# Where a transform group takes its PSUM banks: the two banks of the x products in mid-step, or one of them and a scratch bank at the step's end

## The chip, the cores and the metric

The kernel runs on one core of a Trainium2 chip. The metric is device time in microseconds. The engines are named as in the profile: PE is TensorE (its matmuls), PEld its weight loads, DVE VectorE, ACT ScalarE, POOL GpSimd, SP SyncE. "L255" is line 255 of the kernel.

## What is computed

```python
# x: (8, 3008, 256)   w_in: (256, 2048)   w_out: (2048, 256), all float32
X = np.fft.fft(x, axis=1)
X = np.fft.fft(X, axis=2)
x = X.real.astype(np.float32).reshape(8 * 3008, 256)
h = x @ w_in
g = h * (1.0 / (1.0 + np.exp(-1.702 * h)))
out = (g @ w_out).astype(np.float32)
```

## The kernel before

All arithmetic is in float32. The Fourier transform over the sequence (3008 = 47 x 64) is done in two stages of matmuls, one batch ahead of the rest; the transform over the 256 features is folded into `w_in` beforehand. What remains is a two-layer network with a gated activation, whose products are cut down by the symmetries of the transform and by Strassen-like combinations.

**Steps.** The network runs in 384 steps t: 8 batches, 3 blocks of a batch, 2 halves of a block, 8 pairs p = t mod 8 of feature blocks. A step with (block 0, half 1) has 226 columns ("narrow"), every other 256 ("wide"). Steps 0 to 7 use a simpler form; from step 8 on a loop written out by hand (`for t in range(n + LAG)`) issues the work, and every engine takes its instructions in that order. LAG is 3: the products with `w_out` of step t - 3 are issued in step t. The parts of a step are these:

- `middle(t)`, ACT, L592, two instructions: writes a bias into the PSUM bank `b{t % 2}`, the bank of x(t).
- `begin(t)` (called P here) and `begin(t, 1)` (called Q), PE, L184 by way of `halves`, output `x`: two groups of eight matmuls each that add the two halves of the products of step t onto that bias. P(t + 1) is issued in the middle of step t, Q(t) at the start of step t.
- `doubled(t)`, ACT, L604: reads x(t) after P. `forward(t)`, ACT, L607: reads x(t) after Q. `backward(t)`, DVE, L565 (one instruction, two in narrow steps): reads x(t) and the result of `doubled`, the last to read the bank. `activate_back(t)`, ACT, L614.
- `sums(t)`, POOL, L622 and L623, and DVE, L629 and L630; `deeper`, DVE, L651: sums from which the products with `w_out` are made. `deeper` follows odd steps.
- `product(t - 3, lo, hi)`, PE, L184, output `o` or `low`: the halves lo to hi of a step's products. From step 8 up to the last eight a step has three halves, of four matmuls each.
- `small_products(t, ks)`, PE, L685: sets of eight small matmuls, only for odd t: sets 1, 2, 4, 7 of t - 3 (`one`) and sets 5, 6, 3 of t - 4 (`other`).
- Once in eight steps a group of outputs is put together: `combine` (ACT L754, L756, DVE L757, L758), `combine_small` (DVE L786, in steps with t mod 8 = 3), `swap` (ACT L794 to L796, three copies, in steps with t mod 8 = 4), `combine_last` (DVE L768, L804).

A step with t mod 8 = 3 is "opening": it issues the first products of an output group.

**Transform groups.** The two stages of the transform for the next batch or block are spread over the steps by a table `extra`, whose entries are called at a step's end. `mix1` (PE L255, 16 to 22 matmuls, two PSUM banks) is followed by two copies by `mixed` (ACT, L263); `stage2` (PE L365, 64 small matmuls, two PSUM banks) by four transposes (DVE, L371). `mix1` needs what `fold1` (POOL, L225 to L231) made. There are 28 `mix1` and, from step 8 on, 23 `stage2`, in 51 steps that the code calls `special`; `after` is a step whose predecessor was special. In batches 1 to 6 (t0 = 48 b) `mix1` comes in steps t0 + 12, 15, 19 and 23, in batch 0 in 16, 20, 25 and 28; `stage2` comes in t0 + 8, 24 and 40.

**Banks.** PSUM has eight banks: two for `o`, three for `low`, `b0` and `b1` for x, and `b2`. A function that asks `bank(name)` without a tag takes the first of the list `spare`. A bank is handed over when the instructions that read its former content are done:

```python
def middle(t):
    x = xb[t] = bank("x", f"b{t % 2}")
    ...
def mix1(b, m):
    ps = [bank("ps1") for _ in range(2)]
    ...                        # matmuls into ps[0] and ps[1] in turn
    waiting.append((m, ps[1]))
    mixed(m, 0, ps[0])
```

Before, a special step s sets `spare` to `b{s % 2}` and `b2`: the group is issued at the end of step s, into the bank of x(s), which `middle(s + 2)` would have taken, and the scratch bank. `middle(s + 2)` is then issued in the after step, behind Q(s + 1). In other steps `middle(t + 2)` is issued in step t.

Of the kernel before, what the change touches and what calls it, by code (L numbers as in the profile page):

```python
# [43 lines left out]
LAG = 3  # L44
# [68 lines left out]
def kernel(ctx: ExitStack, tc, x, w_in, w_out, tab1, tab2, out):  # L113
    nc = tc.nc
# [147 lines left out]
    def mixed(m, r, ps):  # L262
        nc.scalar.copy(free(xt[:], (4 * m + r) * D, [2 * D, 2], [1, D]), free(ps[:], 0, [D, 2], [1, D]))  # L263
# [321 lines left out]
    def middle(t):  # L585

        b, blk, hh, p = steps[t]
        n = width(t)
        x = xb[t] = bank("x", f"b{t % 2}")
        for i in range(2):  # L590
            f = 2 * p + i
            nc.scalar.activation(x[:, i * 256:i * 256 + n], nbt[b, blk][:, hh * 256:hh * 256 + n], ACTF.Copy,  # L592
                                 scale=af1[:, f:f + 1])

    def begin(t, cs=0):

        n = width(t)
        for i in range(2):
            halves(xb[t][:, i * 256:i * 256 + n], *operands(t, cs, i), start=False, stop=(cs == 1))
# [9 lines left out]
    def backward(t):  # L609
        at = at_left(t, A21)  # L610
        reversed_sum(big[:, at:at + 256], at_right(t, A22) - at, gt.pop(t), xb.pop(t), width(t), ALU.subtract)
# [49 lines left out]
    def small_products(t, ks):  # L661

        if t < 0 or not deep(t) or not steps[t][3] % 2:
            return
        p, w = steps[t][3] - 1, width(t) // 2
        for k in ks:
            for pr in range(2):
                for side in range(2):
                    op_ = 2 * pr + side
                    weights, q = ((wo, 2), (wo, 3), (wt, 2), (wt, 3))[op_]  # L670
                    y0, y1 = (weights[:, p + i, q, :] for i in range(2))
                    at = MADE + (p // 2 * 2 + pr) * 512 + side * 64
                    lhs = {1: y0[:, 0:64], 2: y1[:, 0:64], 3: y1[:, 64:128]}.get(k)
                    if lhs is None:
                        at += {5: 0, 6: 1, 7: 2, 4: 3}[k] * 128
                        lhs = big[:, at:at + 64]
                    raw_ = {1: (t - 1, 0), 2: (t, 0), 4: (t, 1)}.get(k)
                    if raw_:
                        rhs = right(raw_[0], op_, 256)[:, raw_[1] * w:raw_[1] * w + w]
                    else:  # L680
                        i0 = SUM + 512 * {5: 0, 6: 1, 7: 2, 3: 3}[k] + 128 * op_
                        rhs = big[:, i0:i0 + w]
                    first_in = p == 0 and (k, pr) in ((2, 0), (2, 1), (4, 1))
                    o = (o_banks[1] if k == 1 else pot["low"])[64 * side:64 * side + 64, spot(pr, k):spot(pr, k) + w]
                    nc.tensor.matmul(o, lhsT=lhs, rhs=rhs, start=first_in, stop=(p == NP - 2), skip_group_check=True)  # L685
# [11 lines left out]
    def product(t, lo, hi):  # L697

        p, n = steps[t][3], width(t)
        if lo == 0 and p == 0:  # L700
            for q in range(2):
                pot[q] = bank(f"po{q}", f"o{q}")
            if t >= NP:
                pot[2] = pot["low"]
            if t >= last:
                pot[3] = bank("po3", "b2")
        if t < NP:

            h = ht[t]
            plan = [(half, dh, wo[:, p, 2 * f + dh, :], h[:, half, f, :n])  # L710
                    for half in range(2) for dh in range(2) for f in range(2)]
        else:
            plan = [(0, 0, wo[:, p, 0, :], left(t, A11, n)), (0, 1, wt[:, p, 0, :], left(t, S2, n)),
                    (1, 0, wt[:, p, 1, :], left(t, S3, n))]
            if not deep(t):
                plan += [(1, 1, wt[:, p, 3, :], right(t, S1, n)), (3, 1, wo[:, p, 3, :], right(t, S4, n)),
                         (3, 0, wo[:, p, 2, :], right(t, A12, n)), (2, 0, wt[:, p, 2, :], right(t, A22, n))]
        todo = plan[lo:hi]

        if t >= len(steps) - 2:  # L720
            if hi:
                return
            pot[t] = plan
            if t == len(steps) - 2:
                return
            todo = [it for pair_ in zip(pot.pop(t - 1), pot.pop(t)) for it in pair_]
        begun = set() if p else pot.setdefault("begun", set())
        for q, i, lhs, rhs in todo:
            halves(pot[q][:, i * 256:i * 256 + n], lhs, rhs, start=(p == 0 and q not in begun), stop=(p == NP - 1))
            begun.add(q)  # L730
        if hi is None and p == 0:
            del pot["begun"]
# [256 lines left out]
    for t in range(n + LAG):  # L989
        if t < NP:  # L990
            if t == NP - 3:
                spare[:] = [tag for tag in spare if tag[0] == "o"] + ["b2"]
            if t == NP - 1:
                middle(NP)
            hidden(t)
            if t == NP - 1:
                begin(NP)
                no_row(1024)
            if t == 0:
                squares(in2, nc.scalar)  # L1000
                nyquist(0, 0)
                low_up(in2)
                low_down(in2)
            if t in rows_at:
                first_row(rows_at[t])
            if t >= LAG and t != LAG + 1:
                product(t - LAG, 0, None)
            if t == LAG:
                product(1, 0, None)
            if t == 5:  # L1010
                bounds(("out", 2))
            if t == 6:
                low_down(("out", 3))
            if t:
                activate(t - 1)
            if t == 3:
                bounds(("in", 3))
            if t == 5:
                bounds(("out", 3), False)
            if t in early:  # L1020
                fold_w(early[t])
            rows(t)
            if t == NP - 1:
                doubled(NP)
                middle(NP + 1)
        else:
            after, special = (any(fn in (mix1, stage2) for fn, _ in extra.get(k, ())) for k in (t - 1, t))
            if t < n:
                begin(t, 1)
            if t == NP:  # L1030
                activate(t - 1)
            if after and t + 1 < n:
                middle(t + 1)
            if t < n:
                forward(t)
            while waiting:
                m, ps = waiting.pop()
                mixed(m, 1, ps)
            opening = (t - LAG) % NP == 0 and t >= NP + LAG
            one, other = (t - LAG, (1, 2, 4, 7)), (t - LAG - 1, (5, 6, 3))  # L1040
            if opening:
                small_products(*other)
            cut = 0 if opening and not after else 3 if after else 2
            product(t - LAG, 0, cut)
            if after:
                small_products(one[0], one[1][:1])
                small_products(other[0], () if opening else other[1][:1])
            if t + 1 < n:
                begin(t + 1)
            if not opening:  # L1050
                small_products(other[0], other[1][after:])
            product(t - LAG, cut, 6 if t - LAG == last else None)
            small_products(one[0], one[1][after:])
            swap(t - LAG - 2)
            if t < n:
                backward(t)
            if t + 1 < n:
                doubled(t + 1)
            if t < n:
                activate_back(t)  # L1060
                sums(t, nc.gpsimd)
            if t + 2 < n and not special:
                middle(t + 2)
            combine_small(t - LAG - 1)
            if t - LAG == last:
                product(last, 6, None)
            sums(t - 1, nc.vector)
            deeper(t - 2, 0)
            deeper(t - 3, 1)
        if t == NP:  # L1070
            psu.close()
            low = ctx.enter_context(tc.tile_pool(name="low", bufs=1, space=PS))
            pot["low"] = low.tile([128, 3 * 512], F32, tag="low", name="low")
        if t >= LAG:
            combine(t - LAG)
            combine_last(t - LAG - 2)
            turn_last(t - LAG - 3, 0)
            turn_last(t - LAG - 4, 1)
        if t >= NP:
            spare[:] = [f"b{t % 2}"] * special + ["b2"]  # L1080
        for fn, args in extra.get(t, ()):
            fn(*args)


# [26 lines left out]
```

## Time and profile before

| what | value |
|---|---|
| median of 3 runs | 1856.31 us (1854.34 to 1856.57) |
| profiled execution: span, first to last instruction | 1853.1 us |
| median of the runs less this span | 3.2 us (the profile gives no time of its own around the span) |
| TensorE busy / weight loads | 1836.6 us (99%) / 1401.3 us (76%) |
| VectorE, ScalarE, GpSimd busy | 82%, 62%, 53% |
| granted TensorE clock, mean | 0.999 |
| mean DMA rate | 57 GB/s |

The span is what the profiler saw between the first and the last instruction of one execution. Busy time of TensorE is taken from pipelined matmuls, so it tells whether it waited, not how fast it went. A row of the timeline has start, duration, engine, line, operation, output and inputs, shapes and, in brackets, the idle time of the engine just before with what ended it. A row of the waits has who waited for whom, and the total, the number of times and the longest.

### The profile page before, as it was taken

To read this page: it belongs to the slowest core of one execution; us is meant where nothing else is said; L and a number is where in the kernel's file an instruction comes from. 1 tells how busy PE (TensorE), PEld (TensorE's weight loads), DVE (VectorE), ACT (ScalarE), POOL (GpSimd) and SP (SyncE) were. 2 spreads that over 40 slices of the span, in tenths; PEclk is the share of its full clock that TensorE was granted. 3 is DMA by queue.
4 is the path that set the end of the run, shared out by engine and by line. 5 is a ranking of instruction groups with operands and counts; after the bars stand their busy time and mean duration, and the time that the engine had idled before them with its cause. 6 is when DMAs were issued, how large, how long until landed. Compare 5 with 4: busy or idle time off the path is not lost.

```text
span 1853.1 us, 56093 instructions
## 1 busy us (share of the span) xinstructions
PE 1836.6 (99%) x23722; PEld 1401.3 (76%) x23722; DVE 1520.9 (82%) x2222; ACT 1150.5 (62%) x2241; POOL 975.2 (53%) x1053
## 2 busy tenths in 40 slices
PE   8999999999999999999999999999999999999998
PEld 4677777777777777777777777777777777778776
DVE  6988778887798778987789878888888888878874
ACT  5666656665666666666566666666665666656663
POOL 4776446744368434773348643485445754444442
PEclk9999999999999999999999999999999999999999
DMA  8721340215012240223302132121411111100111
GB/s 280 181 61 34 85 67 19 72 52 99 19 46 48 73 81 13 52 50 90 57 13 67 43 86 52 19 75 35 103 31 23 37 46 36 31 19 13 23 19 24
DMA packets 149707, 105.31 MB, mean 57 GB/s; under 512 B 106057, under 2 KB 130665, under 8 KB 148896
## 3 DMA queue, kind: packets, MB, share of 16 engines
q1 hardware_dynamic: 146624, 99.68, 23.6%
q8 instruction: 187, 3.06, 0.7%
q10 hardware_dynamic: 2832, 2.05, 0.5%
q14 instruction: 64, 0.52, 0.1%
HBM read 64.41 MB, written 48.05 MB: 61 GB/s over the span
## 4 chain that ended last, share of the span: by engine, by line
PE 80%; DVE 9%; POOL 4%; ACT 2%; DMA 2%; issue 2%; SPq 0%; DVEq 0%; ACTq 0%; POOLq 0%
PE x L184 29%; PE o L184 22%; PE low L685 21%; PE o L685 3%; DVE big L651 3%; PE ps L255 2%; DVE big L786 2%; DVE big L565 1%; PE ps L365 1%; POOL xt L227 1%; DVE big L629 1%; POOL big L623 1%; DMA xt<-in_x_dram 1%; ACT big L607 1%; DMA Td<-big 1%
## 5 line engine op out<-in xcount | busy, mean ns | idle before, releaser
L622 POOL TENSOR_TENSOR big<-big 128x256 f32<-128x256 f32 (+1 forms) x376 | 353.0, 939 | 825.1 <-ACT big L614 691.4
L184 PE MATMUL x<-pq,wcs 128*64 128x256 f32 (+1 forms) x6016 | 768.8, 376 | 2.0 <-ACT g L604 1.4
L651 DVE TENSOR_TENSOR big<-big 128x512 f32<-128x512 f32 (+1 forms) x736 | 623.1, 861 | 23.4 <-PE low L685 4.7
L184 PE MATMUL o<-big,wo 128*64 128x256 f32 (+1 forms) x4800 | 620.8, 375 | 0.1
L184 PEld LDWEIGHTS x<-pq,wcs 128*64 128x64 f32 x6016 | 412.3, 137 | 186.0 <-issue 15.0
L184 PEld LDWEIGHTS o<-big,wo 128*64 128x64 f32 x4800 | 341.6, 137 | 148.0 <-DVE big L629 0.5
L604 ACT ACTIVATE g<-x 128x512 f32<-128x512 f32 (+1 forms) x376 | 221.6, 589 | 366.3 <-PE x L184 365.0
L565 DVE TENSOR_TENSOR big<-g,x 128x512 f32<-128x512 f32 (+2 forms) x440 | 254.1, 589 | 209.4 <-ACT big L607 209.0
L592 ACT ACTIVATE x<-nb,af 128x256 f32<-128x256 f32 (+1 forms) x752 | 352.9, 469 | 79.7 <-DVE pq L371 63.6
L685 PE MATMUL low<-big 128*64 128x128 f32 (+1 forms) x5888 | 382.8, 270 | 0.0
L685 PEld LDWEIGHTS low<-big 128*64 128x64 f32 x5888 | 337.5, 137 | 29.2
L623 POOL TENSOR_TENSOR big<-big 128x256 f32<-128x256 f32 (+1 forms) x376 | 352.6, 938 | 0.0
L607 ACT ACTIVATE big<-x 128x512 f32<-128x512 f32 (+1 forms) x376 | 219.2, 583 | 127.5 <-PE x L184 121.3
L614 ACT ACTIVATE big<-big 128x512 f32<-128x512 f32 (+1 forms) x376 | 231.9, 617 | 46.0 <-DVE big L565 44.0
L685 PE MATMUL low<-big,wo 128*64 128x128 f32 (+1 forms) x2944 | 220.4, 271 | 0.1
L685 PEld LDWEIGHTS low<-big,wo 128*64 128x64 f32 x2944 | 171.3, 137 | 4.2 <-DVE big L651 1.4
L630 DVE TENSOR_TENSOR big<-big 128x512 f32<-128x512 f32 (+1 forms) x188 | 160.8, 855 | 6.5
L629 DVE TENSOR_TENSOR big<-big 128x512 f32<-128x512 f32 (+1 forms) x188 | 137.3, 730 | 5.3 <-POOL big L622 5.3
L786 DVE TENSOR_TENSOR big<-big,low 128x512 f32<-128x512 f32 (+3 forms) x184 | 109.0, 609 | 3.5
L685 PEld LDWEIGHTS o<-big,wo 128*64 128x64 f32 x1472 | 92.2, 137 | 25.0
L685 PE MATMUL o<-big,wo 128*64 128x128 f32 (+1 forms) x1472 | 110.0, 270 | 0.0
L227 POOL TENSOR_TENSOR xt<-xt 111x510 f32<-111x510 f32 x56 | 86.0, 1535 | 4.4
(95 smaller groups left out, 966.2 us busy)
## 6 DMA issues: line engine op xcount, KB each, us to landing
out_dram<-os SPq DMA_DIRECT2D x284, 64.0 KB
t<-Td SPq DMA_DIRECT2D x22, 512.0 KB
Td<-xt SPq DMA_DIRECT2D x56, 192.0 KB
xt<-in_x_dram SPq DMA_DIRECT2D x14, 512.0 KB
xt<-Xr SPq DMA_DIRECT2D x14, 512.0 KB
nb<-Nd SPq DMA_DIRECT2D x23, 256.0 KB
out_dram<-os SPq DMA_DIRECT2D x96, 56.0 KB
Xr<-in_x_dram SPq DMA_DIRECT2D x7, 752.0 KB
```

What stands on the lines that cost most here:

```text
L184: nc.tensor.matmul(out[c0:c0 + 64], lhsT=lhs[:, c0:c0 + 64], rhs=rhs, skip_group_check=True, **how)
L565: nc.vector.tensor_tensor(free(out, at + m - 1, [by, 2], [RUN, blocks], [-1, m]), *ins, op=op)
L592: nc.scalar.activation(x[:, i * 256:i * 256 + n], nbt[b, blk][:, hh * 256:hh * 256 + n], ACTF.Copy, scale=af1[:, f:f + 1])
L604: nc.scalar.activation(two(g[:], n), two(xb[t][:], n), ACTF.Copy, scale=2.0)
L607: nc.scalar.activation(front(t), two(xb[t][:], width(t)), ACTF.Gelu_apprx_sigmoid)
L614: nc.scalar.activation(back(t), back(t), ACTF.Gelu_apprx_sigmoid)
L622: eng.tensor_tensor(right(t, S1, n), left(t, A21, n), right(t, A22, n), op=ALU.add)
L623: eng.tensor_tensor(left(t, S3, n), left(t, A11, n), left(t, A21, n), op=ALU.subtract)
L629: eng.tensor_tensor(s2, s1, a11, op=ALU.subtract)
L630: eng.tensor_tensor(s4, a12, s2, op=ALU.subtract)
L651: nc.vector.tensor_tensor(out, i0, i1, op=how)
L685: nc.tensor.matmul(o, lhsT=lhs, rhs=rhs, start=first_in, stop=(p == NP - 2), skip_group_check=True)
```

## The change

In a special step s the group is no longer called at the step's end from `extra`, but in mid-step: behind Q(s), three product halves (one in an opening step, in which the `other` sets come ahead) and one set of small products. `backward(s)`, `activate_back(s)` and POOL's `sums(s)` are issued ahead of it. The group takes `b{(s + 1) % 2}` and `b{s % 2}`. Behind it come `middle(s + 1)` and the second `mixed`, the rest of the small products and halves, and then P(s + 1), at the step's end. The step ahead of a special one (`apart`) issues no `middle` for s + 1 any more. In an after step two product halves go ahead of Q. At the end of a step `spare` is `b2` alone.

```diff
             after, special = (any(fn in (mix1, stage2) for fn, _ in extra.get(k, ())) for k in (t - 1, t))
-            if t < n:
+            apart = any(fn in (mix1, stage2) for fn, _ in extra.get(t + 1, ()))
+            opening = (t - LAG) % NP == 0 and t >= NP + LAG
+            one, other = (t - LAG, (1, 2, 4, 7)), (t - LAG - 1, (5, 6, 3))
+            if t == NP:
                 begin(t, 1)
-            if t == NP:
                 activate(t - 1)
-            if after and t + 1 < n:
-                middle(t + 1)
+            elif t < n and not after:
+                begin(t, 1)
+            if opening:
+                small_products(*other)
+            if after:
+                product(t - LAG, 0, 2)
+                begin(t, 1)
             if t < n:
                 forward(t)
-            while waiting:
-                m, ps = waiting.pop()
-                mixed(m, 1, ps)
-            opening = (t - LAG) % NP == 0 and t >= NP + LAG
-            one, other = (t - LAG, (1, 2, 4, 7)), (t - LAG - 1, (5, 6, 3))
-            if opening:
-                small_products(*other)
-            cut = 0 if opening and not after else 3 if after else 2
-            product(t - LAG, 0, cut)
-            if after:
+            cut = 1 if opening and special else 3 if after or special else 0 if opening else 2
+            product(t - LAG, 2 if after else 0, cut)
+            if special:
+                if not opening:
+                    small_products(other[0], other[1][:1])
                 small_products(one[0], one[1][:1])
-                small_products(other[0], () if opening else other[1][:1])
-            if t + 1 < n:
+                backward(t)
+                activate_back(t)
+                sums(t, nc.gpsimd)
+                spare[:] = [f"b{(t + 1) % 2}", f"b{t % 2}"]
+                for fn, args in extra[t]:
+                    if fn in (mix1, stage2):
+                        fn(*args)
+                middle(t + 1)
+                while waiting:
+                    m, ps = waiting.pop()
+                    mixed(m, 1, ps)
+            elif t + 1 < n:
                 begin(t + 1)
             if not opening:
-                small_products(other[0], other[1][after:])
+                small_products(other[0], other[1][special:])
             product(t - LAG, cut, 6 if t - LAG == last else None)
-            small_products(one[0], one[1][after:])
+            small_products(one[0], one[1][special:])
+            if special:
+                begin(t + 1)
             swap(t - LAG - 2)
-            if t < n:
+            if t < n and not special:
                 backward(t)
             if t + 1 < n:
                 doubled(t + 1)
-            if t < n:
+            if t < n and not special:
                 activate_back(t)
                 sums(t, nc.gpsimd)
-            if t + 2 < n and not special:
+            if t + 2 < n and not apart:
                 middle(t + 2)
             combine_small(t - LAG - 1)
...
         if t >= NP:
-            spare[:] = [f"b{t % 2}"] * special + ["b2"]
+            spare[:] = ["b2"]
         for fn, args in extra.get(t, ()):
-            fn(*args)
+            if t < NP or fn not in (mix1, stage2):
+                fn(*args)
```

## The prediction

> **What bounds the kernel now.** I read the page first, then the waits, then the timeline of two special steps. A *special* step is one that carries a transform group (`mix1`, L255, or `stage2`, L365); the step behind it is *after*.
>
> The head of the page:
>
> ```profile
> span 1853.1 us, 56093 instructions
> PE 1836.6 (99%) x23722; PEld 1401.3 (76%) x23722; DVE 1520.9 (82%) x2222; ACT 1150.5 (62%) x2241; POOL 975.2 (53%) x1053
> PEclk9999999999999999999999999999999999999999
> ```
>
> TensorE is the bound, at full clock. Its real pace is in the start-to-start times of the timeline: eight x products (256 columns) 0.87 us, one product half (4 matmuls) 0.43, one set of eight small products 0.437; at 226 columns 0.76, 0.38, 0.385. Two ordinary steps hold 32 x, 24 product and 56 small matmuls: 3.48 + 2.61 + 3.06 = 9.15 us; by the starts of `begin(t, 1)` they last 4.77 + 4.33 = 9.10 us. So nothing is lost there, and any wait of TensorE adds to the end whole.
>
> The waits (total us, times, longest) name the one place where a transform group already waits:
>
> ```profile
> PEld x L184 <- ACT x L592: 8.6, 33, 0.7
> PE ps L255 <- DVE big L565: 2.5, 5, 0.5
> ```
>
> The second row is seen in the timeline of step 60, whose `begin(60, 1)` starts at 325.50 (start, us, engine, line, shapes):
>
> ```profile
> 325.50 0.93 PE L184 MATMUL x<-pq,wcs 128*64 128x226 f32 x8
> ...
> 326.79 2.85 DVE L651 TENSOR_TENSOR big<-big 128x452 f32<-128x452 f32 x3
> ...
> 328.41 0.62 ACT L796 COPY big<-big 64x512 f32<-64x512 f32 x1
> ...
> 328.94 0.94 PE L685 MATMUL low<-big 128*64 128x113 f32 x16
> ...
> 329.56 0.68 DVE L565 TENSOR_TENSOR big<-g,x 128x448 f32<-128x448 f32 x2
> ...
> 330.39 0.29 PE L255 MATMUL ps<-e,w 47*64 47x129 f32 x1 [0.50 <-DVE big L565]
> ...
> 332.03 0.59 ACT L263 COPY xt<-ps 128x512 f32<-128x512 f32 x1 [1.17 <-DMA Xr<-in_x_dram]
> 332.50 1.10 PEld L184 LDWEIGHTS o<-big,wo 128*64 128x64 f32 x12
> 332.65 0.94 ACT L592 ACTIVATE x<-nb,af 128x226 f32<-128x226 f32 x2
> ```
>
> The group needs the bank of x(60), which is free when `backward(60)` (L565) has read it, at 330.24. VectorE gets to it late: three L651 (`deeper`) stand before it until 329.6. The last matmul before the group starts at 329.62, so TensorE stands still for half a microsecond. After the group ACT copies the bank out (332.03) and writes the bias (`middle`, L592) only then.
>
> The timeline of step 88, a `stage2`, has the same chain over VectorE:
>
> ```profile
> 462.43 1.16 PE L365 MATMUL ps<-t,small 64*32 64x128 f32 x64
> 463.52 0.63 PEld L184 LDWEIGHTS x<-pq,wcs 128*64 128x64 f32 x8 [0.20 <-issue]
> 463.52 1.08 PE L184 MATMUL x<-pq,wcs 128*64 128x256 f32 x8
> 463.63 1.44 DVE L371 STREAM_TRANSPOSE pq<-ps 128x256 f32<-128x256 f32 x4 [1.67 <-PE ps L365]
> 464.22 1.22 PEld L184 LDWEIGHTS o<-big,wo 128*64 128x64 f32 x12
> 464.43 1.47 PE L184 MATMUL o<-big,wo 128*64 128x256 f32 x12
> 464.53 0.99 ACT L592 ACTIVATE x<-nb,af 128x256 f32<-128x256 f32 x2 [2.98 <-DVE pq L371]
> ```
>
> TensorE does not feel these chains today, because it has Q (0.87), three halves (1.3) and often a small set (0.44) to do before the next P needs the bias: 2.35 to 2.65 us lie between the starts of Q(s+1) and P(s+2) in all 51 pairs.
>
> **The change, part by part.** No matmul, copy or transpose is added (one early bias write, 0.98 us of ACT at step 8, aside); everything is order and banks. For a special step s, measured from the start of Q(s):
>
> *1. The group arrives sooner.* TensorE now has only Q(s), three halves and one small set before it: 0.87 + 1.30 + 0.44 = 2.61 us (226 columns: 0.76 + 1.15 + 0.38 = 2.29). Before, it also had P(s+1) and the rest of the small sets: the matmul ahead of the group starts at 3.75 to 4.8. The group's second bank is that of x(s), so it still waits for `backward(s)`; what is queued behind it on TensorE is everything. The trace gives the end of L565 after Q(s) for each kind, 0.14 us from there to the first matmul (330.24 to 330.39):
>  - `mix1` at s mod 8 = 4 (20, 28, and 60, 108, 156, 204, 252, 300): 4.75 in five, 4.07 (252), 5.02 (20), 3.97 (28). Here the group starts when it starts now, 4.89, but with 1.15 + 0.76 = 1.9 us of matmuls (the small sets and P) not yet done that are done now. Six narrow steps lose 1.9 each; step 20 loses 2.2, step 28 1.4 (its group starts 0.76 sooner than now).
>  - `mix1` at s mod 8 = 7 (12 steps): L565 ends at 3.3 to 3.43, once at 2.46; arrival 2.29 or 2.61. The wait is 0 to 1.2; VectorE, late from steps before, will have caught up while TensorE stood at the specials before, so I take 0.4.
>  - `mix1` at s mod 8 = 3 (6 steps): 2.46 against 2.62: none.
>  - `stage2` (23 steps, s mod 8 = 0): 2.31 to 2.48 against 2.61 or 2.29: none, 0.1 in the seven narrow ones. In six (72, 120, ...) that follow a special step, Q comes two halves later, arrival is 0.87 + 0.43 + 0.44 = 1.74 after it, and L565 can't end before about 2.0: 0.4. Step 8 has 4.03: 1.9.
>  - Steps 16 and 25: 0.1 and 1.3.
>
> *2. P(s+1) stands behind the group.* Its bias waits for the copy out. For `mix1`, step 60 gives: next matmul possible 331.88, first L592 done 333.10, so 1.3 us must be covered. The cover is three small sets (1.15 or 1.31) where s is even, two (0.87) or two halves (0.87) where it is odd: a loss of 0.1, and 0.46 (0.56 narrow). For `stage2`, step 88 gives 463.52 and first L592 done 465.01, with the second 0.51 later: 1.6 to cover, by 1.31 (1.15 narrow): 0.3 (0.46).
>
> *3. ACT in the mod-4 steps.* `swap` (L794 to L796, 0.62 each) now queues behind the copies of the group, and `doubled(s+1)` and `middle(s+2)` behind it. From the group's last matmul start: 0.46 to the copy, then copy 0.62, bias 0.97, copy 0.62, swap 1.95, doubled 0.58, first bias 0.48, in all 5.7 us. TensorE has 0.31 (exit) + 1.15 + 0.18 (part 2) + P 0.76 + two halves 0.76 + Q 0.76 + a half 0.38 = 4.3. So P(s+2) waits 1.4 (1.0 wide). The other kinds have no swap: `middle(s+2)` is ready 1.4 us after P(s+1) and 2.2 us of matmuls cover it; without that cover it would cost that 1.4.
>
> *4. The after step* has its Q behind two halves: nothing waits for it for two steps. Now after steps take 4.82 and 4.44 where ordinary ones take 4.77 and 4.33, so up to 0.1 each in 51 might go. I credit 2.5 us, half. The bank b2 freed from the groups gains nothing: no row waits for it. ACT's bias write moved out of the step ahead was beside other work. GpSimd's folds, needed by `mix1`, end at most 1.6 us after Q(s) (step 16; 0.06 elsewhere), before arrival. SP's transfers keep their places.
>
> Sum: mod 4: 6 x (1.9 + 1.4) + (2.2 + 1.0) + (1.4 + 1.0) = 25.4. Mod 7: 12 x (0.4 + 0.5) = 10.8. Mod 3: 6 x 0.46 = 2.8. `stage2`: 1.9 + 7 x 0.56 + 6 x 0.7 + 9 x 0.3 = 12.7. Steps 16 and 25: 1.8. Together 53.5, less 2.5: +51 us on the profiled 1853.1, so 1904. The median of the runs, 1856.3, lies 3.2 above this span, for what the span leaves out: 1907.
>
> The clock: today's longest stand-still inside the program, 1.17 us near 25.7 us of the span, passed at a granted clock of 1.00 (mean of 0 to 30 us); the new ones reach 2.5 us, so the row says full clock only by stretching it. [...]
>
> **Rivals.**
>  - *Milder, same cause* (12%). VectorE and ACT recover during the waits, so that only the group waits of the mod-4 steps (15 us) and a few of part 2 (8) stay: about +20, 1876. For it: ACT is busy 62% only. Against: both queues keep their order, and the terms of part 3 are durations of rows.
>  - *Faster* (5%). `backward(s)` comes in time because ACT has one bias write less ahead of it. Then the wait at step 60 (0.5 us, six times) and the 0.1 of 51 after steps go: 3 + 5 = -8, 1848. It decides at L565 ending by 2.3 us after Q(60); but L565 has no idle time ahead of it on VectorE, and L651, not ACT, is what runs there.
>  - *No difference* (2%): the groups start where they start now, because the waits for `backward` are as long as the work moved behind them everywhere; only gains and losses within 4 us remain. The mod-3 steps, with L565 at 2.46, speak against it.
>  - *Worse* (8%): the late `forward` and `backward` of the after steps push the bias of P(s+3) too; 1 us more in each of 51 pairs would make it +102, 1958.
>
> **How the numbers follow.** The forecast has 73%. Its range: without the swap term (-11), without waits at mod 7 (-5), `stage2` covers holding (-4), the whole 5 us of the after steps (-2.5): +28, 1885. With the full wait at mod 7 (+6), 1 us more at each mod-4 step (+8) and 0.25 more at each `stage2` (+6): +71, 1927. For 8 in 10 I reach down over the milder rival, less the 4 us by which its 8 us of part 2 could be halved: 1872 to 1927. A difference under 0.2% (3.7 us) is about what can't be told from none: faster 5%, same 2%, slower 93%.
>
> **What would show it.** In the profile after: a new large row PE or PEld ps L255 waiting for DVE big L565, about 20 us; the row x L184 waiting for ACT x L592 grown from 8.6 to some 25 to 35; TensorE's busy share lower by 2 to 3 points; step 60 with its group at about 4.9 us after Q and P(62) waiting over 1 us. Wrong if L565 of step 60 ends by 2.5 us after Q, if the L592 wait doesn't grow, or if TensorE's busy share is still 99%.

## The result, and the profile after

The changed kernel takes 1922.24 us (median; 1922.18 to 1923.77) against 1855.7 us: the ratio is 1.0362, 95% interval 1.0348 to 1.0377. It is slower by 66.5 us, where +51 was forecast. The profiled span is 1920.4 us, 67.3 more than before.

The head of the page after:

```profile
span 1920.4 us, 56096 instructions
PE 1861.4 (97%) x23722; PEld 1401.2 (73%) x23722; DVE 1518.2 (79%) x2222; ACT 1163.8 (61%) x2243; POOL 967.7 (50%) x1053
```

The work is the same (23722 matmuls; ACT has two bias writes more); TensorE is idle for 59 us instead of 16.5. The waits of TensorE after (total us, times, longest):

```profile
PEld x L184 <- ACT x L592: 46.1, 79, 1.2
PEld x L184 <- ACT g L604: 29.0, 57, 1.7
PE x L184 <- ACT x L592: 25.7, 49, 0.8
PE x L184 <- ACT g L604: 8.9, 8, 1.3
PEld ps L255 <- DVE big L565: 6.2, 8, 2.2
PE ps L365 <- DVE big L565: 2.8, 7, 1.5
PE ps L255 <- DVE big L565: 2.3, 2, 1.7
```

The weight loads (PEld) show a longer wait than the matmuls do, because they run ahead of them: before P(61), shown below, the loads had ended at 343.80 and the matmuls at 344.02. The two are not to be added. Three waits are there: x products for the bias (L592), x products for `doubled` (L604), and the groups for `backward` (L565).

The timeline of step 60 after, whose Q starts at 337.24, shows all three:

```profile
337.24 0.93 PE L184 MATMUL x<-pq,wcs 128*64 128x226 f32 x8
337.92 2.77 DVE L651 TENSOR_TENSOR big<-big 128x452 f32<-128x452 f32 x3
...
339.63 0.32 PE L255 MATMUL ps<-e,w 47*64 47x129 f32 x1
...
340.62 0.68 DVE L565 TENSOR_TENSOR big<-g,x 128x448 f32<-128x448 f32 x2
...
341.40 0.43 PE L255 MATMUL ps<-xt,w 47*64 47x256 f32 x2 [1.12 <-issue]
...
343.41 0.94 ACT L592 ACTIVATE x<-nb,af 128x226 f32<-128x226 f32 x2
...
344.40 0.98 PE L184 MATMUL x<-pq,wcs 128*64 128x226 f32 x8 [0.38 <-ACT x L592]
344.87 0.62 ACT L794 COPY big<-big 64x512 f32<-64x512 f32 x1
...
346.81 0.55 ACT L604 ACTIVATE g<-x 128x452 f32<-128x452 f32 x1
...
347.41 0.98 PE L184 MATMUL x<-pq,wcs 128*64 128x226 f32 x8 [1.26 <-ACT g L604]
```

The group's first four matmuls go into the free bank at 339.63; those for the bank of x(60) start at 341.40, 0.1 us after L565 ends (341.30). The page puts this wait down to "issue", so the L565 rows above are too small. P(61) starts at 344.40, 53 ns after the *second* L592 ends, and Q(61) at 347.41, 53 ns after L604 ends, which stands behind `swap`.

Step 88 after, a lone wide `stage2`:

```profile
479.74 1.16 PE L365 MATMUL ps<-t,small 64*32 64x128 f32 x64
...
481.83 0.99 ACT L592 ACTIVATE x<-nb,af 128x256 f32<-128x256 f32 x2 [1.67 <-DVE pq L371]
...
482.87 1.08 PE L184 MATMUL x<-pq,wcs 128*64 128x256 f32 x8 [0.51 <-ACT x L592]
```

The group itself doesn't wait here; P(89) does, again to the end of the second L592 (482.82).

To see where the 67 us lie, I compare pairs: the time from the start of Q(s) to that of Q(s + 2), after less before, summed by kind.

| kind | forecast, us | measured, us |
|---|---|---|
| mod 4: 6 narrow, 20, 28 | 25.4 | 24.4 |
| mod 7 and the six `stage2` behind them | 15.0 | 24.0 |
| mod 3 | 2.8 | 5.4 |
| lone `stage2`, 8 wide and 7 narrow | 6.3 | 11.3 |
| step 8 | 1.9 | 1.6 |
| 16; 24 and 25 | 2.1 | 2.8 |
| all other steps, start and end | -2.5 | -2.2 |

### The profile page after: what moved, and what is told of

Its sections match the earlier page's. It is cut to its first block, busy times and chain, and to the rows that moved or that the text cites. A ratio compares the mean times of both kernels' runs of the same rounds, so it can differ in the third digit from the quotient of the medians.

```text
span 1920.4 us, 56096 instructions
## 1 busy us (share of the span) xinstructions
PE 1861.4 (97%) x23722; PEld 1401.2 (73%) x23722; DVE 1518.2 (79%) x2222; ACT 1163.8 (61%) x2243; POOL 967.7 (50%) x1053
## 4 chain that ended last, share of the span: by engine, by line
PE 86%; ACT 6%; DVE 4%; DMA 2%; issue 1%; SPq 0%; POOL 0%; ACTq 0%; DVEq 0%; POOLq 0%
PE x L184 33%; PE o L184 24%; PE low L685 21%; PE o L685 4%; ACT x L592 3%; PE ps L255 2%; PE ps L365 1%; ACT xt L263 1%; DVE pq L371 1%; DMA xt<-in_x_dram 1%; DVE big L651 1%; DVE big L565 1%; ACT g L604 0%; DVE big L786 0%; ACT big L607 0%
## 5 line engine op out<-in xcount | busy, mean ns | idle before, releaser
L622 POOL TENSOR_TENSOR big<-big 128x256 f32<-128x256 f32 (+1 forms) x376 | 347.9, 925 | 900.1 <-ACT big L614 754.6
L184 PEld LDWEIGHTS x<-pq,wcs 128*64 128x64 f32 x6016 | 411.7, 137 | 231.6 <-ACT x L592 46.1
L565 DVE TENSOR_TENSOR big<-g,x 128x512 f32<-128x512 f32 (+2 forms) x440 | 254.5, 590 | 251.0 <-ACT big L607 250.7
L604 ACT ACTIVATE g<-x 128x512 f32<-128x512 f32 (+1 forms) x376 | 221.8, 590 | 351.6 <-PE x L184 350.3
L592 ACT ACTIVATE x<-nb,af 128x256 f32<-128x256 f32 (+1 forms) x754 | 353.9, 469 | 51.0 <-DVE pq L371 37.7
L623 POOL TENSOR_TENSOR big<-big 128x256 f32<-128x256 f32 (+1 forms) x376 | 367.5, 977 | 0.0
L629 DVE TENSOR_TENSOR big<-big 128x512 f32<-128x512 f32 (+1 forms) x188 | 131.8, 701 | 2.3 <-POOL big L622 2.3
L227 POOL TENSOR_TENSOR xt<-xt 111x510 f32<-111x510 f32 x56 | 77.4, 1382 | 4.4
```

The lines of the kernel that those rows point to most:

```text
L184: nc.tensor.matmul(out[c0:c0 + 64], lhsT=lhs[:, c0:c0 + 64], rhs=rhs, skip_group_check=True, **how)
L565: nc.vector.tensor_tensor(free(out, at + m - 1, [by, 2], [RUN, blocks], [-1, m]), *ins, op=op)
L604: nc.scalar.activation(two(g[:], n), two(xb[t][:], n), ACTF.Copy, scale=2.0)
L622: eng.tensor_tensor(right(t, S1, n), left(t, A21, n), right(t, A22, n), op=ALU.add)
L623: eng.tensor_tensor(left(t, S3, n), left(t, A11, n), left(t, A21, n), op=ALU.subtract)
L629: eng.tensor_tensor(s2, s1, a11, op=ALU.subtract)
```

## Experiments

The theory after the result: the loss is a sum of waits that come from the order and the banks, namely the group for `backward(s)`, P(s + 1) for the later of the two bias writes, and Q(s + 1) for `doubled(s + 1)`. The rival, which no row had shown: the place in mid-step itself costs, whatever the banks. Each run was timed beside the kernel before, whose median lay between 1854.57 and 1856.17 in these sessions; a saving "against the changed kernel" is between medians of two sessions, so some 1.6 us of it may be their difference. A gain of a pair is read from the traces. The changed kernel lies at 1.0362.

**The group in the scratch bank.**

```diff
-                spare[:] = [f"b{(t + 1) % 2}", f"b{t % 2}"]
+                spare[:] = [f"b{(t + 1) % 2}", "b2"]
```

> The changed kernel, but the group's second bank is the scratch bank b2 instead of that of x(s), so that the group needn't wait for backward(s). Theory (four waits: the group for backward, P(s+1) for both bias writes, Q(s+1) for doubled behind swap, and small change of order): the wait of ps L255 and ps L365 for DVE L565 goes, but the copy out stands behind activate_back(s) on ACT, which itself waits for backward(s), so in the mod-4 steps 0.8 of 1.5 us comes back, 0.6 in the six stage2 steps that follow a special one, 0.5 at steps 71, 119, ..., 1 at step 8: about -13 us against the changed kernel, 1909. Rival (the place in mid-step itself costs, by draining the array twice more, whatever the banks): -2 at most, 1920.

1910.98 us, ratio 1.0297 (1.0282 to 1.0313): 11 us less. The pairs of narrow mod-4 steps gain 0.98 to 1.01, the chains from 71, 119, ... 0.6 to 0.9, step 8 1.56; the lone pairs outside mod 4 gain nothing. No group waits inside any more, and the bias waits grow, as they should where ACT's `activate_back` still waits for `backward`:

```profile
PE x L184 <- ACT x L592: 34.5, 51, 2.0
```

**`swap` ahead of the group.**

```diff
             if special:
                 ...
+                swap(t - LAG - 2)
                 backward(t)
                 ...
-            swap(t - LAG - 2)
+            if not special:
+                swap(t - LAG - 2)
```

> The changed kernel, but swap is issued ahead of backward(s), activate_back(s) and the group in a special step, so that doubled(s+1) doesn't stand behind it on ACT. Theory: in the mod-4 steps (60, 108, ..., 28) Q(s+1) waits 1.3 us for doubled(s+1); this goes, 7 x 1.25 = -9 us, 1913, and the other special steps, which have no swap, don't move. Rival (mid-step place): 0, 1922.

1915.68 us, ratio 1.0327 (1.0309 to 1.0344): 6.6 us less. Four narrow mod-4 pairs gain 1.32, step 28 1.22, step 20 0.11, the pairs without `swap` nothing. Two, 108 and 300, gain 0.28 and 0.43 only. The windows of step 108 say why; columns are the busy time of each engine, then the granted clock:

```profile
571.40:573.30 1.90, 0.78 (x12) 0.27 (x9) 1.87 (x5) 1.30 (x3) 1.74 (x2) 1.00 0.23 39
573.30:574.50 1.20, 1.20 (x19) 0.81 (x19) 1.17 (x3) 0.47 (x1) 0.65 (x1) 1.00 0.88 255
574.50:578.07 3.57, 3.57 (x34) 3.04 (x35) 2.90 (x3) 2.01 (x4) 3.49 (x4) 0.54 0.27 97
```

TensorE stood still for 1.12 us up to 573.26, and from 574.8 the clock was halved for 3.41 us (0.54 in the mean of 574.50 to 578.07, 0.98 in the next 2.93 us). I return to this at the end.

**The bias a step earlier.** The group takes b2 and the bank of x(s), so that the bank of x(s + 1) is free for its bias all the time.

```diff
-                spare[:] = [f"b{(t + 1) % 2}", f"b{t % 2}"]
+                spare[:] = ["b2", f"b{t % 2}"]
 ...
-                middle(t + 1)
 ...
-            if t + 2 < n and not apart:
+            if t + 2 < n:
                 middle(t + 2)
```

> The changed kernel, but the group takes b2 and the bank of x(s), and middle(s+1) is issued a step earlier, as in any other step; P(s+1) stays behind the group at the step's end. Theory: P(s+1) then waits for no bias; by the trace of the changed kernel its starts stand 0.4 to 1.1 us behind the matmul before in special steps, and these sum to some 30 us over the ordinary 0.2; with the bias gone from ACT's queue doubled comes 0.9 sooner in the mod-4 steps, 3 us more: -33 us, 1889. By the prediction's own term (P waits for the first bias write alone) it would be -17, 1905. Rival (mid-step place): 0 to -5.

1883.09 us, ratio 1.0146 (1.0131 to 1.0161): 39 us less, the largest of the single edits and a little more than the 33 expected. Lone `stage2` pairs gain 0.69 and 0.74 and stand within 0.06 of before; mod 3 gains 0.96 and is even with before. The wait for the bias is back at the size it had before (8.6):

```profile
PEld x L184 <- ACT x L592: 7.9, 31, 0.6
```

By the starts, the waits of P(s + 1) beyond the ordinary 0.2 us fall from 29.5 us to 0.1, and those of Q(s + 1), which wait for `doubled`, from 13.4 to 9.1. The prediction's own price for the first, 17, doesn't fit.

**Q first in the after steps.**

```diff
-            elif t < n and not after:
+            elif t < n:
                 begin(t, 1)
 ...
             if after:
                 product(t - LAG, 0, 2)
-                begin(t, 1)
```

> The changed kernel, but Q goes first in the after steps again, ahead of the two product halves. Theory: Q(s+1) writes the bank that doubled(s+1) reads, and starts 53 ns after its end in the trace of the changed kernel; with P(s+1) at the end of step s nothing then covers P's end (0.36), doubled (0.6) and the hand-overs (0.1): 0.9 us more in each of 51 pairs, +46 us, 1968. By the prediction's part 4 (nothing waits for Q, so its place matters by 0.1 at most): 0 to +5, 1922 to 1927.

1962.62 us, ratio 1.0575 (1.0559 to 1.0591): 40 us more than the changed kernel. All kinds lose, the lone `stage2` pairs 0.86 each:

```profile
PE x L184 <- ACT g L604: 47.4, 51, 2.0
```

Once in each of the 51 pairs Q waits for `doubled`. The two halves ahead of Q are what covers this in the changed kernel.

**The bias written by two engines.** In `mix1` steps VectorE writes the second half.

```diff
+            if i and not both_:          # mix1 steps only
+                nc.vector.tensor_scalar(x[:, 256:256 + n], nbt[b, blk][:, hh * 256:hh * 256 + n], scalar1=af1[:, f:f + 1],
+                                        scalar2=None, op0=ALU.mult)
+                continue
```

> The changed kernel, but in the 28 mix1 steps the second half of the bias of x(s+1) is written by VectorE (one tensor_scalar with the same factor), beside ACT's first half. Theory (P waits for the later of the two writes): both are done about 0.45 us after the copy out instead of 0.94, so P(s+1), or Q(s+1) behind swap, comes 0.4 to 0.5 sooner in the mix1 steps: about -12 us against the changed kernel, 1910; VectorE now stands still until the copy, which may give back a few. By the prediction's term (the first write alone counts): 0, 1922.

1922.13 us, ratio 1.0360 (1.0344 to 1.0375): no change in all. The parts differ: four narrow mod-4 pairs gain 0.47 to 0.49, as ACT has one write less ahead of `swap` and `doubled` (the other two have a halved clock; the mean of the run is 0.998), the mod-3 pairs gain 0.05, the chains from 71, 119, ... lose 0.3 in the mean and step 8 loses 0.8. As a test of the price of P's wait it fails, since the second write doesn't run beside the first. The timeline of step 67 (in this kernel L596 is ACT's write, L593 VectorE's):

```profile
376.82 0.48 ACT L596 ACTIVATE x<-nb,af 128x256 f32<-128x256 f32 x1
...
377.33 0.49 DVE L593 TENSOR_SCALAR x<-nb,af 128x256 f32<-128x256 f32 x1 [2.41 <-ACT x L596]
...
377.87 1.08 PE L184 MATMUL x<-pq,wcs 128*64 128x256 f32 x8 [0.74 <-DVE x L593]
```

VectorE waits until ACT's half is done (377.30), and P until VectorE's is (377.82), though the first four of its matmuls touch only ACT's half. So P waits here for whoever writes the bank last. In the list of instructions only the first of P's matmuls carries a wait, one for both halves; that the program could do without it is likely, but wasn't tried.

**Bias early and `swap` first together.** The edits of the second and third run.

> The edits of the two runs before this together: bias a step earlier with banks b2 and that of x(s), and swap ahead of the group. Theory: only the wait of the group for backward(s) stays (mod-4 steps, the stage2 steps behind a special one, step 8). Q(61) still waits about 0.9 us for doubled(61) with the bias early alone; this goes in seven steps: -6 us against that kernel, 1877, which is +21 over the kernel before. Rival (mid-step place costs by itself): the two savings overlap, 1883.

1877.58 us, ratio 1.0124 (1.0105 to 1.0143): 5.5 us less than with the bias early alone. Five of six narrow mod-4 pairs now stand at 0.8 to 1.6 over before; the sixth, 300, at 2.48 with the halved clock (mean of the run 0.998). What remains is in mod 4, in the six chains that start at 71, 119, ... (8.3 together) and in step 8, all of which have L565 late.

**P ahead of the group too.**

```diff
             if special:
                 ...
+                begin(t + 1)
                 swap(t - LAG - 2)
                 backward(t)
 ...
-            if special:
-                begin(t + 1)
```

> As the run with both edits, but P(s+1) is also issued ahead of the group; of the change then remain the place in mid-step, with the rest of the small products behind it, and the two halves ahead of Q in the after steps. Theory: the group comes 0.76 to 0.87 later, so it waits less for backward(s) and keeps less work behind it; what stays is about 0.5 us in six mod-4 steps, 1.4 and 0.4 at 20 and 28, 0.8 at step 8, less 1.6 that the changed kernel gains outside: +4 over the kernel before, 1860. Rival (mid-step place costs by itself): it stays at 1870 or above.

1868.65 us, ratio 1.0071 (1.0056 to 1.0086): 9 less again, but 14 over before instead of 4. The narrow mod-4 pairs do better than expected: five of six are within 0.08 of before, where 0.5 was expected, and step 252 keeps 1.38. Steps 20 and 28 keep 1.24 and 0.34, as expected. The lone `stage2` pairs, at 0.06 until now, stand at 0.38 (wide) and mostly 0.55 (narrow), with a new wait in step 89:

```profile
468.77 1.44 DVE L371 STREAM_TRANSPOSE pq<-ps 128x256 f32<-128x256 f32 x4 [2.30 <-PE ps L365]
...
470.14 0.65 DVE L629 TENSOR_TENSOR big<-big 128x512 f32<-128x512 f32 x1
...
470.85 0.65 PE L184 MATMUL o<-big,wo 128*64 128x256 f32 x4 [0.22 <-DVE big L629]
```

The second product half needs what L629 makes. L629 was queued behind the transposes, which wait for the group while VectorE is idle for 2.30 us; and with P gone from the step's end TensorE arrives sooner. It is the change's own move of the group ahead of `sums(t - 1)` on VectorE, hidden until then by longer waits.

**VectorE's sums ahead of the transposes.**

```diff
                 backward(t)
+                sums(t - 1, nc.vector)
 ...
-            sums(t - 1, nc.vector)
+            if not special:
+                sums(t - 1, nc.vector)
```

> As the run before (both edits, P ahead of the group), but in special steps VectorE's sums(t-1) (L629, L630) are issued right behind backward(s), ahead of the four transposes of the group. In that run the second product half of the after step waits for L629, which stands behind the transposes while VectorE is idle for 2.3 us ahead of them; 0.38 us are lost in wide stage2 pairs, 0.55 in narrow ones, 0.43 in the six pairs behind a special step. Theory: these go, 8 x 0.38 + 7 x 0.5 + 6 x 0.43 = -9 us, 1859 to 1860, +4 over the kernel before, from steps 8, 20, 252 and the narrow mod-7 steps. Rival (mid-step place costs by itself): 1868, unchanged.

1863.65 us, ratio 1.0044 (1.0031 to 1.0058): 5 less, not 9. In the wide steps the theory holds: lone wide `stage2` pairs are now 0.06 *below* before, those behind a special step even with it, and mod 3 is 0.1 below. Six of the seven narrow ones got worse, most of them from 0.55 to 1.11 over before. Step 56 shows why:

```profile
312.12 0.72 POOL L623 TENSOR_TENSOR big<-big 128x256 f32<-128x256 f32 x1
312.19 2.57 DVE L629 TENSOR_TENSOR big<-big 128x512 f32<-128x512 f32 x1 [0.51 <-POOL big L622]
312.81 0.72 POOL L230 TENSOR_TENSOR xt<-xt 111x254 f32<-111x254 f32 x1
313.50 0.72 POOL L231 TENSOR_TENSOR xt<-xt 111x254 f32<-111x254 f32 x1
```

L629, 0.68 us in the median, takes 2.57 here and in the five others that got worse, each time beside three GpSimd instructions in a row; the transposes stand behind it, and P(58) then waits 0.90 for its bias. What is left over before is in these narrow pairs (6.4 us), in mod 4 (3.2, most of it at 20 and 252), in the narrow mod-7 pairs (1.5, where the weights of Q(s + 1) still wait 0.43 for `doubled`) and at step 8 (0.7). With this the place in mid-step is cleared: where no wait is left, the pairs are at or below those of before. These gain about 1.2 us in all (8 x 0.06 + 6 x 0.1 + 0.15 at step 16), under 0.1%, so no version that beats the kernel before by a measurable amount is in sight, and none was built.

## Why the prediction was right, and where its sizes were off

**Right in kind and sign.** The special steps lose because TensorE stands still in them, and the rest of the kernel moves by 2 us. The group of step 60 was forecast at 4.9 us after Q; the part that needs the bank of x(60) starts at 341.40 - 337.24 = 4.16, because L565 ended at 4.06 there, as it did before only in step 252. That the mod-4 sum came out at 24.4 against 25.4 is in part luck: in the narrow steps `backward` came 0.7 us sooner than in five of six before, and P(s + 1) waited 0.44 us beyond the ordinary instead of the 0.1 of my sum.

**Part 2, the mis-sized term.** I let P start when the first L592 is done, and took the second as covered by P's first matmuls. In 49 of 51 steps P starts 52 to 53 ns after the *second* ends. This is one L592, 0.45 to 0.48 us, in almost every special step. By the starts of P, the waits beyond the ordinary 0.2 sum to 29.5 us after, where my terms give about 17. That is 12 of the 16 us by which the span was missed; the rest isn't split further. It is seen in mod 3 (0.9 a pair instead of 0.46), in mod 7 and in `stage2` (0.79 instead of 0.3). The third run gave back 39 us when the bias had no copy to wait for. No row of before had shown P starting between the two writes; the value was chosen, not read. The trace of before did hold the answer: in steps 10, 13, 25 and 351 P starts 53 to 54 ns after the second write, and in no step ahead of its end.

**Part 3: right size, wrong place.** I let P(62) wait 1.4 us behind `swap`. It is Q(61) that waits, 1.26, because Q writes into the bank that `doubled` reads. The second run removed 1.32 a pair. The chain on ACT is the one that I had added up; that it gave the same size with another instruction at its end is luck.

**Part 4 was a mistake that cost nothing.** "Nothing waits for Q" is true, but Q waits for `doubled`, and with P at the step's end this needs a cover of 0.9 us. The two halves that the change puts there are that cover; the fourth run took them away and lost 40 us. The credit of 2.5 us appeared as -2.2 in the other steps, not as the cheaper after steps that I had argued, and 0.6 of it fell ahead of step 8, where the two kernels do the same: that it fits is luck.

**Part 1.** The arrivals were right (1.7 to 2.5 us from Q to the last matmul ahead of the group) and so was the reason. The group's own waits, by the starts of its matmuls, grew from 3 to 15 us. The wait at mod 7 was nothing in the narrow steps (L565 ends at 2.30, as VectorE had caught up) and about the 0.4 that I took stayed in the wide ones (L565 ends at 3.33 in five of six, and their groups have a gap of 0.41 to 0.42 us between two starts).

**The rivals.** The milder case is excluded, ACT did not recover. The faster one would have needed L565 within 2.3 us of Q(60); it came at 4.06. No difference and the worse case (+102) are excluded by the 66.5 us. These lie inside the range, but near its upper end of 71, for which I had added 6, 8 and 6 us at mod 7, mod 4 and `stage2`. What came was 9 at mod 7, 5 at the lone `stage2`, 3 at mod 3 and nothing at mod 4, most of it from the bias: that the range held is partly luck. The clock is no rival: the one drop in the changed kernel's steps, 3.41 us at half rate, costs at most an estimated 1.7 us, half of its length. The check points: TensorE's share fell by 2 points and the weight loads' L592 row rose from 8.6 to 46.1, above the 25 to 35 that I gave, by the same undersized term. The ps-L565 rows, for which I foretold 20 us, show 2 to 6 at a time, because part of that wait is booked as "issue"; by the starts it is the 15 us above, still under 20.

## What to carry to other kernels

When work moves, ask of each instruction behind it which wait it carries now, and until when: here a consumer waited for the last write of the bank as the program counts it (P started 52 to 53 ns after the second L592 in 49 of 51 steps), and a writer for the last reader (Q(61) 53 ns after `doubled`). A queue that stands idle for a distant producer (VectorE ahead of the transposes, 2.30 us in step 88 of the run with P ahead) delays what is listed behind (there L629, and with it a product half by 0.22), and such a wait may show only after a larger one is gone. Compare stretches of the trace that hold the same work, by starts, kind by kind: they gave each edit's worth to 0.05 us where the totals only gave a sum.

## What the runs showed of the hardware

The clock of TensorE was halved behind some of the new waits, so the row of before, 1.17 us at a granted clock of 1.00, could not be stretched to all of them. The kernel before has no gap over 0.9 us in its steps and no low clock until its end (1.00 from 30 to 1840 us). In the run with the bias early all six narrow mod-4 steps have a gap of 1.11 to 1.12 us; after one of them, step 108, the clock went down, 1.2 us after work had begun again (columns as above):

```profile
565.00:567.10 2.10, 1.22 (x18) 0.88 (x18) 2.07 (x6) 0.58 (x1) 1.39 (x2) 1.00 0.71 187
567.10:570.50 3.40, 3.40 (x31) 3.02 (x32) 1.74 (x2) 2.92 (x5) 2.85 (x4) 0.50 0.27 97
```

In the changed kernel it happened once within the steps, at step 20, behind a gap of 1.72 us: half rate for 3.41 us, from 143.95 to 147.36. The 15 other gaps over 0.9 us in its steps, of 0.95 to 1.49 us, were followed by no drop. In the profiled runs of the experiments, whose mean granted clock lay between 0.996 (fourth run) and 1.000 (last), I counted 13 drops within the steps, behind gaps of 1.12 to 2.03 us (once still inside a gap), and none behind most gaps of the same length. In the second run the drop at step 108 cost 1.0 us (0.28 gained instead of 1.32). So the length of a gap does not decide it alone: 1.12 us were followed by a drop in the second run, 1.49 us in the changed kernel by none. What else decides is not shown.

L629 on VectorE took 2.57 us in step 56 of the last run, instead of 0.68, beside a row of three GpSimd instructions of 0.72 us each. It ended 0.54 us after the third of them; no run tested what makes it long.
